# Four value tiles of the first batch by SyncE as f32, the first scores in a new order, and the first unit's output steps regrouped

## The chip, the cores and the metric

The kernel runs on one core of one Trainium2 chip. The metric is the device time of one execution in microseconds (us); of the kernel before there are 4 runs, 260.92 to 262.25 us, median 261.1 us. A profile is one such execution recorded instruction by instruction. Its engines are PE (TensorE matmul; PEld is its weight load), DVE (VectorE), ACT (ScalarE), POOL (GpSimd) and SP (SyncE, which here only issues DMAs). L103 is line 103 of the kernel before.

## The reference, cut to what matters

Shapes: q, k, v are (4 batches, 8 heads, 768 positions, 64), all f32.

```
k_sum = max  of k over blocks of 32 positions      (24 summary keys)
v_sum = mean of v over blocks of 32 positions      (24 summary values)
scores_l = q k^T / 8          only where |i - j| < 16
scores_s = q k_sum^T / 8 + log(32)
a = softmax over [scores_l, scores_s] together
attn = a [v ; v_sum]  ->  x: (3072 tokens, 512)
out = x + sigmoid(x w_res) * ((gelu(x w_gate) * (x w_val)) w_out)
```

w_gate and w_val are 512x1536, w_out 1536x512, w_res 512x512. Matmuls take bf16 operands.

## The kernel before, in words

**Units.** A unit is half a batch: 384 tokens. There are 8 units, u = 0 to 7. Work is issued in the order in which the code stands; there is no scheduler that would move it, and each engine works through its own instructions in that order. An instruction that waits holds up everything behind it on its engine.

**Attention on tiles of 64 positions.** `vext` (L78) holds for each of the 12 tiles of a batch 96 rows that go with its 64 queries (64 own values, 16 after, 16 before) and 32 more rows for the block means; columns D to VP of a tile (64 to 95) hold a column of ones for the softmax sum and zeros. `kW` (L75) holds the matching keys and `qT` the queries, both with the 64 features on partitions. `s_step` (L289) makes the scores of one pair of heads and their exponentials P; `av_step` (L312) multiplies P by `vext`; `xt_step` (L342) turns the result into `xT`, the operand of the dense layers. A pair of heads is "hp", 0 to 3.

**Dense part.** `fo_step` (L371) makes one of 12 column blocks of gate and value products on PE (lines 357 to 361, 4+4 matmuls of 128x384), gelu on ACT (L365), the product on DVE (L366). `res_step` (L394) makes a residual product for 128 tokens and its tanh on ACT; `ffn_step` (L403) the product with w_out, in parts over fo; `end_step` (L423) joins them and stores. The output steps of unit u are interleaved with the attention of unit u+1: in `first_out` (L521) for unit 0, `mid_out` (L553) for the others. w_gate and w_val come in 6 chunks of 256 columns each, so a chunk serves two fo.

**The start.** POOL loads with a cast from f32 to bf16, in this order: two halves of the keys (`k_sb`, L88), the first queries (`q_sb`, L96), 6 value tiles, four mask instructions (L176), 6 more value tiles (L103), then the weights (L189, L190, with the second queries L192 after the fifth pair), w_res, two shifted copies within `vext` (L194), w_out in three parts (L198), and the next batch. POOL has at most 8 such loads open: the compiled order shows each one waiting for the landing of the eighth before it. PE turns keys and queries (L205), ACT copies them out of PSUM (L237, L244), DVE forms the block maxima and the shifted rows of `kW` (L222 to L231). PE runs `keep_warm` (L437), matmuls on a dummy tile, where it would otherwise have nothing to do. `vsum_mm` (L247) makes the block means of the first batch on PE from all 12 value tiles, two matmuls a tile, spread between the score steps (lines 461 to 465); `vblk` (L466, L468) takes them. ACT's first work is to fill the pad columns of `vext[0]` (L168), DVE fills those of `vext[1]` (L182).

**Later batches.** `vsum_grp` (L254) makes the means on PE, DVE copies them to `vpart`, four small DMAs on SP move them to the rows of `vsum` (L264), and POOL spreads them over `vext` (L270). `turn_q` (L130) is a transposing DMA on SP.

`unit0_extras` (L505) is housekeeping done on DVE between the fo steps of unit 0. The order of the first scores reads:

```
        s_step(0, 0, st)
        q_place(0, 3, tq[3])
        s_step(0, 1, st, MM2)
...
        vsum_mm(0, vs, 0, 3)
        s_step(0, 2, st)
        vsum_mm(0, vs, 3, 5)
        s_step(0, 3, st, MM2)
        vsum_mm(0, vs, 5, NT)
```

Of the kernel before, what the change touches and what calls it, by code (L numbers as in the profile page):

```python
# [8 lines left out]
F32 = mybir.dt.float32  # L9
# [6 lines left out]
def kernel(  # L16
# [84 lines left out]
    def v_loads(b, lo=0, hi=NT):  # L101
        for t in range(lo, hi):
            nc.gpsimd.dma_start(out=vext[b % 2][0:QT, t, :, 0:D],  # L103
                                in_=v[b, :, t * QT:(t + 1) * QT, :].rearrange("h p d -> p h d"))
# [30 lines left out]
    with tc.manual_schedule():  # L135
# [13 lines left out]
        def own_keys(m, n):  # L149
            nc.vector.memset(m[:], 0.0)  # L150
            for i in range(2):
                rows = m[i * BLK:(i + 1) * BLK]
                nc.vector.memset(bass.AP(tensor=m.tensor, offset=rows[:, 0, i:i + 1].offset,
                                         ap=[rows.ap[0], [34, n]]), 1.0 / BLK)

        nc.vector.memset(warm[:], 0.0)
        nc.vector.memset(ident[:], 0.0)
        nc.vector.memset(bias_t[:], 0.0)
# [6 lines left out]
                                base=0, pattern=[[-1, 128]], channel_multiplier=1)  # L165
        load_k(0, k_sb[0], 1, 2)
        q_sb[0] = load_q(0, QJ)
        nc.scalar.activation(vext[0][0:QT, :, :, D + 1:VP],  # L168
                             warm[0:QT, 0:1].unsqueeze(1).unsqueeze(1).to_broadcast([QT, NT, H, VP - D - 1]),
                             AF.Copy)  # L170
        vext_consts(0)
        v_loads(0, 0, 6)
        for cols, sign, base in ((slice(0, QT), 1, WIN - 1), (slice(0, QT), -1, WIN - 1),
# [1 line left out]
            m = mneg[0:QT, cols]  # L175
            nc.gpsimd.affine_select(out=m, in_=m, compare_op=ALU.is_ge, fill=-240000.0, base=base,  # L176
                                    pattern=[[-sign, cols.stop - cols.start]], channel_multiplier=sign)
        v_loads(0, 6, NT)
        kw_consts(0)
        own_keys(bmat, NT)  # L180
        nc.vector.memset(vblk[96:128, :, D:D + 1], 1.0)
        nc.vector.memset(vext[1][0:QT, :, :, D + 1:VP], 0.0)  # L182


        wg_src = moe_w_gate.rearrange("(ko ki) f -> ki ko f", ki=128)
# [58 lines left out]
            nc.scalar.copy(qT[0][:, 3 * half:3 * half + 3, hp].rearrange("d c (p j) -> d c p j", j=qj),  # L244
                           tp.rearrange("d j (c p) -> d c p j", c=3))

        def vsum_mm(b, vs, lo, hi):  # L247
            for t in range(lo, hi):
                for i in range(2):
                    nc.tensor.matmul(vs[i][96:128, 0:DM // 2], bmat[:, t, :],  # L250
                                     vext[b % 2][0:QT, t, 4 * i:4 * i + 4, 0:D],
                                     start=(t == 0), stop=(t == NT - 1))

        def vsum_grp(b, pool, tag):  # L254
            vs = pool.tile([128, DM], F32, tag=tag, name="vs")
            for i in range(3):
                for g in range(4):
                    nc.tensor.matmul(vs[32 * g:32 * g + 32, :], bgrp[:, i, :],  # L258
                                     vext[b % 2][0:QT, 3 * g + i, :, 0:D],
                                     start=(i == 0), stop=(i == 2), tile_position=(0, 32 * g),  # L260
                                     skip_group_check=True)
            nc.vector.tensor_copy(vpart[:], vs[:])
            for g in range(4):
                nc.sync.dma_start(out=vsum[b % 2][96 + 6 * g:102 + 6 * g, :],  # L264
                                  in_=vpart[32 * g:32 * g + 6, :])

        def vsum_bc(b, lo, hi, eng):
# [169 lines left out]
        def keep_warm(n):  # L437
            wp = ps_s.tile([128, 2, 512], F32, tag="s", name="wp")
            for _ in range(n):
                nc.tensor.matmul(wp[:, 0], warm[:, 0:128], warm[:], start=True, stop=True)  # L440
# [4 lines left out]
        keep_warm(6)  # L445
        k_step(0, 2, ps_mm, "mm")
        k_step(0, 3, ps_mm, "mm")
        keep_warm(5)
        tq = [turn_pair(q_sb[0], hp, turn_tile(q_sb[0], ps_mm, "mm")) for hp in range(NP)]
        for hp in range(3):  # L450
            q_place(0, hp, tq[hp])
        keep_warm(1)
        st = new_unit()
        vs = [ps_t.tile([128, 512], F32, tag="t", name="vs"), ps_o.tile([128, 512], F32, tag="ao", name="vs")]
        s_step(0, 0, st)
        q_place(0, 3, tq[3])
        s_step(0, 1, st, MM2)
        x = vext[0]
        nc.vector.tensor_copy(x[QT:BAND, 1:HT, :, 0:D], x[QT - 2 * WIN:QT, 0:HT - 1, :, 0:D])
        nc.vector.tensor_copy(x[QT:QT + WIN, 0:HT, :, 0:D], x[0:WIN, 1:HT + 1, :, 0:D])  # L460
        vsum_mm(0, vs, 0, 3)
        s_step(0, 2, st)
        vsum_mm(0, vs, 3, 5)
        s_step(0, 3, st, MM2)
        vsum_mm(0, vs, 5, NT)
        nc.vector.tensor_copy(vblk[96:128, 0:H // 2, 0:D],  # L466
                              vs[0][96:128, 0:DM // 2].rearrange("p (h d) -> p h d", d=D))
        nc.scalar.copy(vblk[96:128, H // 2:H, 0:D],  # L468
# [36 lines left out]
        def unit0_extras(fo):  # L505
            if fo == 2:
                mt = ps_o.tile([128, 128], BF16, tag="ao", name="mt")
                nc.tensor.transpose(mt[:], mneg[:], ident[:])
                nc.vector.tensor_scalar(out=maskt[:], in0=mt[:, 0:QT], scalar1=-1.0, scalar2=None,
                                        op0=ALU.is_ge)  # L510
                own_keys(bgrp, 3)
            elif fo == 3:
                kw_consts(1)
            elif fo < 7:
                vsum_bc(0, 2 * fo - 2, 2 * fo, nc.vector)
            elif fo == 7:
                vext_consts(1)
            elif fo < 10:
                nc.vector.memset(vsum[fo - 8][96:128, :], 0.0)

        def first_out(u, st, gvT, nst):  # L521
            n = u + 1
            other = dict(pool=ps_t, tag="t")
            turn = dict(pool=ps_t, tag="t", copy=nc.scalar.copy)
            s_step(n, 0, nst)
            s_step(n, 1, nst, TO2)
            res_step(st, 0)
            res_step(st, 1)
            ffn_step(st, gvT, 0, 0, 4)
            av_step(n, 0, nst)  # L530
            av_step(n, 1, nst, **other)
            s_step(n, 2, nst)
            ffn_step(st, gvT, 1, 0, 4)
            res_step(st, 2)
            ffn_step(st, gvT, 2, 0, 4)
            xt_step(n, 0, nst, **turn)
            av_step(n, 2, nst)
            s_step(n, 3, nst)
            ffn_step(st, gvT, 0, 4, 8)
            ffn_step(st, gvT, 1, 4, 8)  # L540
            xt_step(n, 1, nst, **turn)
            ffn_step(st, gvT, 2, 4, 8)
            av_step(n, 3, nst)
            xt_step(n, 2, nst, **turn)
            ffn_step(st, gvT, 0, 8, FO)
            end_step(u, st, 0)
            ffn_step(st, gvT, 1, 8, FO)
            xt_step(n, 3, nst, **turn)
            ffn_step(st, gvT, 2, 8, FO)
            end_step(u, st, 1)  # L550
            end_step(u, st, 2)
# [39 lines left out]
        for u in range(NU):  # L591
            b, half = u // 2, u % 2
            nb = b + 1
            if half == 0 and nb == 1:
                k_sb[nb] = k_tile()
                load_k(nb, k_sb[nb], 0, 1)
                v_loads(nb)
                load_q_nat(nb)
            if u:
                gvT = upool.tile([128, FO, TU], BF16, tag="gvT", name="gvT")  # L600
            for fo in range(0 if u else 2, FO):
                if u > 1 and fo == 0:
# [12 lines left out]
                if half == 0 and 1 < nb < B and fo == 0:  # L615
                    pool_after(st["xT"][0:1, KO - 1, 0:1])
                    k_nat = load_k_nat(nb)
                    v_loads(nb)
                if half == 0 and b and fo == 1:
                    v_rims(b, HT, NT)  # L620
                if half == 0 and 1 < nb < B and fo == 6:
                    turn_k(nb, k_nat)
                    k_rims(nb, slice(0, NP), nc.gpsimd)
                if half == 1 and nb < B:
                    if fo == 0:
                        v_rims(nb, 0, HT)
                        if nb > 1:
                            pool_after(st["xT"][0:1, KO - 1, 0:1])
                            load_q_nat(nb)
                    if fo == (4 if nb == 1 else 1):  # L630
                        vsum_grp(nb, ps_t, "t")
                        for i in range(4):
                            vsum_bc(nb, 3 * i, 3 * i + 3, nc.gpsimd)
                        turn_q(nb, 0)
                        turn_q(nb, 1)
                    if nb == 1:
                        if fo == 0:
                            tk = turn_all(k_sb[nb])
                        if fo < NP:
                            k_place(nb, fo, tk[fo])  # L640
                    elif 2 <= fo < 2 + NP:
                        k_blocks(nb, fo - 2)
            if u == NU - 1:
                last_out(u, st, gvT)
            else:
                nst = new_unit()
                (mid_out if u else first_out)(u, st, gvT, nst)
                st = nst
# [30 lines left out]
```

## Time and profile before

| what | value |
|---|---|
| time of 4 runs | 260.92 to 262.25 us, median 261.1 us |
| time of the profiled execution | 260.92 us |
| its span, first to last instruction | 259.0 us |
| PE busy | 249.8 us (96%) |
| DVE, ACT, POOL busy | 156.2, 126.0, 104.3 us |
| granted TensorE clock | 0.996 |
| mean DMA rate | 114 GB/s (29.61 MB) |

The 1.92 us between time and span lie around the recorded instructions. PE is busy for 96% of the span, but that counts the dummy matmuls of `keep_warm`, so a busy PE in the first 21 us isn't a PE with useful work. The rows of a timeline read: start in us, duration in us, engine, line, operation, output<-inputs, how many instructions are merged in the row, and in brackets the idle time of the engine before the row with what ended it. In the rows by stretch each engine's busy time stands beside its name, then the granted clock, then "DMA share" (above 1, several packets lie in one DMA engine at once) and the rate.

### The profile page before, as it was taken

The numbers are of one execution on the slowest core, as the hardware profiler recorded it, in microseconds if no ns is written. First come the engines' busy times: TensorE is split into PE (matmuls) and PEld (weight loads), VectorE is DVE, ScalarE is ACT, GpSimd is POOL, SyncE is SP. The second block draws the span as 40 slices with busy tenths as digits, with TensorE's granted clock in tenths as the row PEclk, the third lists the DMA queues.
The fourth block names the chain that finished last, engine by engine and source line by source line (L and its number), as shares of the span: only waits on it lengthen the run. The fifth ranks groups of instructions, "written<-read, shape, count | busy, mean of one in ns | idle before, by whom it ended". The sixth has DMA issues, their size and how long they took to land.

```text
span 259.0 us, 5828 instructions
## 1 busy us (share of the span) xinstructions
PE 249.8 (96%) x2306; PEld 138.6 (54%) x2306; DVE 156.2 (60%) x346; ACT 126.0 (49%) x210; POOL 104.3 (40%) x142
## 2 busy tenths in 40 slices
PE   6999997999999999999999999999999999999993
PEld 2565653565654565545654565546554665456543
DVE  5945763489568544667667544778666544854324
ACT  6685347556383437543393338343482337343310
POOL 8896454285170888243530987153620000000000
PEclk9999999999999999999999999999999999999998
DMA  5999999999943999979903999969803400240012
GB/s 83 177 121 170 197 215 206 199 166 173 90 91 62 178 128 136 123 133 168 142 0 65 200 116 151 113 130 164 134 16 107 104 0 3 48 138 0 0 40 85
DMA packets 98299, 29.61 MB, mean 114 GB/s; under 512 B 83384, under 2 KB 95104, under 8 KB 98160
## 3 DMA queue, kind: packets, MB, share of 16 engines
q0 software_dynamic: 68400, 14.96, 71.3%
q1 hardware_dynamic: 29872, 14.29, 25.0%
q8 instruction: 18, 0.29, 0.5%
q14 instruction: 9, 0.07, 0.1%
HBM read 29.36 MB, written 6.29 MB: 138 GB/s over the span
## 4 chain that ended last, share of the span: by engine, by line
PE 80%; DMA 11%; POOL 3%; ACT 2%; DVE 1%; issue 1%; POOLq 0%; DVEq 0%
PE f L408 23%; PE g L360 22%; PE vv L360 21%; PE r L398 7%; DMA w_val<-in_moe_w_val_dram 4%; DMA w_gate<-in_moe_w_gate_dram 3%; DMA q_sb<-in_q_dram 3%; PE ao L320 3%; PE s L284 2%; POOL vext L103 1%; PE vs L258 1%; DVE P L306 1%; DMA out_dram<-o 1%; ACT P L302 1%; POOL w_val L190 1%
## 5 line engine op out<-in xcount | busy, mean ns | idle before, releaser
L366 DVE TENSOR_TENSOR gvT<-ge,vv 128x384 bf16<-128x384 f32 x96 | 52.9, 553 | 50.9 <-PE vv L360 46.3
L365 ACT ACTIVATE ge<-g 128x384 f32<-128x384 f32 x96 | 47.0, 491 | 74.2 <-DVE gvT L366 41.3
L360 PE MATMUL vv<-xT,w_val 128*128 128x384 bf16 x384 | 78.8, 326 | 0.5 <-DMA w_val<-in_moe_w_val_dram 0.5
L360 PE MATMUL g<-xT,w_gate 128*128 128x384 bf16 x384 | 78.8, 326 | 0.3
L408 PE MATMUL f<-w_out,gvT 128*128 128x512 bf16 x276 | 64.9, 380 | 1.3 <-ACT th L401 1.3
L360 PEld LDWEIGHTS <-w_gate 128*128 128x128 bf16 x384 | 37.1, 98 | 26.5 <-issue 1.6
L360 PEld LDWEIGHTS <-w_val 128*128 128x128 bf16 x384 | 37.4, 98 | 25.6 <-DMA w_val<-in_moe_w_val_dram 1.1
L408 PEld LDWEIGHTS <-gvT 128*128 128x128 bf16 x276 | 25.7, 98 | 30.8 <-DMA w_out<-in_moe_w_out_dram 1.8
L103 POOL DMA_DIRECT2D vext<-in_v_dram x48 | 32.7, 724 | 13.2 <-DMA w_out<-in_moe_w_out_dram 5.7
L401 ACT ACTIVATE th<-r 128x512 f32<-128x512 f32 x24 | 13.6, 605 | 28.4 <-PE r L398 28.4
L414 DVE SCALAR_TENSOR_TENSOR th<-th,f 128x512 f32<-128x512 f32 (+2 forms) x26 | 16.7, 641 | 15.4 <-PE f L408 15.4
L270 POOL COPY vext<-vsum 32x1536 bf16<-32x1536 bf16 x12 | 17.1, 1464 | 21.7 <-DMA vsum<-vpart 21.7
L306 DVE TENSOR_TENSOR P<-P,maskt 128x768 bf16<-128x768 bf16 x28 | 16.7, 601 | 11.6 <-ACT P L302 7.0
L398 PE MATMUL r<-w_res,xT 128*128 128x512 bf16 x96 | 23.2, 380 | 0.4 <-DMA w_res<-in_moe_w_res_dram 0.4
L302 ACT ACTIVATE P<-s,bias_t 128x768 bf16<-128x768 f32 x17 | 15.3, 901 | 6.6 <-PE s L284 6.4
L340 DVE TENSOR_TENSOR xn<-ao,rz 128x384 bf16<-128x384 f32 x32 | 17.8, 558 | 1.1
L417 DVE SCALAR_TENSOR_TENSOR o<-th,xn 128x512 f32<-128x512 f32 (+2 forms) x26 | 17.4, 669 | 1.5 <-DMA out_dram<-o 0.6
L117 POOL DMA_DIRECT2D k_nat<-in_k_dram x24 | 16.4, 741 | 1.0 <-DMA k_nat<-in_k_dram 0.7
L123 POOL DMA_DIRECT2D q_nat<-in_q_dram x18 | 15.9, 911 | 0.8 <-issue 0.7
L299 ACT ACTIVATE P<-s,bias_t 128x384 bf16<-128x384 f32 x30 | 15.7, 578 | 0.3 <-PE s L284 0.3
L222 DVE TENSOR_REDUCE ks<-kW 128x24 bf16<-128x768 bf16 x16 | 15.1, 945 | 0.4 <-ACT kW L237 0.3
L398 PEld LDWEIGHTS <-xT 128*128 128x128 bf16 x96 | 8.9, 98 | 10.3 <-issue 0.3
(82 smaller groups left out, 164.8 us busy)
## 6 DMA issues: line engine op xcount, KB each, us to landing
out_dram<-o SPq DMA_DIRECT2D x23, 256.0 KB, 2.3
vext<-in_v_dram POOLq DMA_DIRECT2D x48, 64.0 KB, 6.4
q_nat<-in_q_dram POOLq DMA_DIRECT2D x18, 128.0 KB, 7.1
w_gate<-in_moe_w_gate_dram POOLq DMA_DIRECT2D x6, 256.0 KB, 8.7
w_val<-in_moe_w_val_dram POOLq DMA_DIRECT2D x6, 256.0 KB, 9.5
w_out<-in_moe_w_out_dram POOLq DMA_DIRECT2D x3, 512.0 KB, 12.4
k_nat<-in_k_dram POOLq DMA_DIRECT2D x24, 64.0 KB, 4.4
vext<-vext SPq DMA_DIRECT2D x6, 144.0 KB, 5.4
```

The source lines that it names most:

```text
L103: nc.gpsimd.dma_start(out=vext[b % 2][0:QT, t, :, 0:D], in_=v[b, :, t * QT:(t + 1) * QT, :].rearrange("h p d -> p h d"))
L270: eng.tensor_copy(vext[b % 2][96:128, lo:hi, :, 0:D], src)
L302: nc.scalar.activation(P.rearrange("p a t q -> p a (t q)"), s2[:, :, 0:TU], AF.Exp, scale=scale, bias=bias_t[:])
L306: nc.vector.tensor_mul(Pf, Pf, maskt.unsqueeze(1).to_broadcast([128, 2 * HT, QT]))
L340: nc.vector.tensor_mul(xn, ao[:, :, :, 0:D], rz.to_broadcast([128, NSUB, 2, D]))
L360: nc.tensor.matmul(ps[:, 0:TU], w[:, ko, fo * 128:(fo + 1) * 128], st["xT"][:, ko, :], start=(ko == 0), stop=(ko == KO - 1), skip_group_ch ...
L365: nc.scalar.activation(ge[:], g[:, 0:TU], AF.Gelu)
L366: nc.vector.tensor_mul(gvT[:, fo, :], ge[:], vv[:, 0:TU])
L398: nc.tensor.matmul(r[:], st["xT"][:, ko, ss], w_res[:, ko, :], start=(ko == 0), stop=(ko == KO - 1))
L408: nc.tensor.matmul(st["f", sub][:], gvT[:, fo, ss], w_out[:, fo, :], start=(fo == 0), stop=(fo == FO - 1), skip_group_check=True)
L414: nc.vector.scalar_tensor_tensor(th[:, cs], th[:, cs], 1.0, f[:, 0:n], ALU.add, ALU.mult)
L417: nc.vector.scalar_tensor_tensor(o.rearrange("p (k d) -> p k d", d=128), th[:, cs].rearrange("p (k d) -> p k d", d=128), 0.5, x, ALU.mult, ...
```

## The change

Seven edits, none of which alters what is computed:

1. Value tiles 8 to 11 of batch 0 are no longer loaded by POOL. SP loads them at the very start, as f32, into a new tile `v32` (tiles 8 and 10 in partitions 0 to 63, 9 and 11 in 64 to 127), with two DMAs of 256 KB. ACT copies tiles 8 and 10 into `vext[0]` as bf16, ahead of its first copy of keys; DVE copies 9 and 11, ahead of its first block maximum.
2. The pad columns of `vext[0]` are zeroed by DVE, from column D rather than D+1, instead of by ACT; DVE's fill of `vext[1]` moves from the start into unit 0, in two halves (fo 3 and 7), and two other fills move one fo later.
3. The block means start with tiles 8 to 11, ahead of the turning of the queries; two of five dummy matmuls there go. The other 8 tiles follow in two groups of 4.
4. The scores of head pairs 2 and 3 are issued one right after the other.
5. In `first_out` the three residual steps stand together after the first two score steps, and the three first parts of `ffn_step` after the next attention steps.
6. The small DMAs of `vsum_grp` are issued by POOL instead of SP.
7. `turn_q` is issued ahead of `vsum_grp`, and for batch 1 both come at fo 5 instead of 4.

```diff
+        v32 = qk.tile([128, 2, H, D], F32, tag="k_nat", name="v32")
+        for i in range(2):
+            nc.sync.dma_start(out=v32[:, i],
+                              in_=v[0, :, (8 + 2 * i) * QT:(10 + 2 * i) * QT, :].rearrange("h p d -> p h d"))
         nc.vector.memset(warm[:], 0.0)
...
-        nc.scalar.activation(vext[0][0:QT, :, :, D + 1:VP],
-                             warm[0:QT, 0:1].unsqueeze(1).unsqueeze(1).to_broadcast([QT, NT, H, VP - D - 1]),
-                             AF.Copy)
+        nc.vector.memset(vext[0][0:QT, :, :, D:VP], 0.0)
         vext_consts(0)
         v_loads(0, 0, 6)
...
-        v_loads(0, 6, NT)
+        v_loads(0, 6, 8)
+        nc.scalar.copy(vext[0][0:QT, 8:NT:2, :, 0:D], v32[0:QT])
         kw_consts(0)
         own_keys(bmat, NT)
         nc.vector.memset(vblk[96:128, :, D:D + 1], 1.0)
-        nc.vector.memset(vext[1][0:QT, :, :, D + 1:VP], 0.0)
+        nc.vector.tensor_copy(vext[0][0:QT, 9:NT:2, :, 0:D], v32[QT:2 * QT])
...
-                                     start=(t == 0), stop=(t == NT - 1))
+                                     start=(t == 8), stop=(t == 7))
...
-                nc.sync.dma_start(out=vsum[b % 2][96 + 6 * g:102 + 6 * g, :],
+                nc.gpsimd.dma_start(out=vsum[b % 2][96 + 6 * g:102 + 6 * g, :],
...
-        keep_warm(5)
+        vs = [ps_t.tile([128, 512], F32, tag="t", name="vs"), ps_o.tile([128, 512], F32, tag="ao", name="vs")]
+        vsum_mm(vs, 8, NT)
+        keep_warm(3)
...
-        vsum_mm(0, vs, 0, 3)
+        vsum_mm(vs, 0, 4)
         s_step(0, 2, st)
-        vsum_mm(0, vs, 3, 5)
         s_step(0, 3, st, MM2)
-        vsum_mm(0, vs, 5, NT)
+        vsum_mm(vs, 4, 8)
...
             elif fo == 3:
                 kw_consts(1)
+                nc.vector.memset(vext[1][0:QT, 0:HT, :, D:VP], 0.0)
             elif fo < 7:
                 vsum_bc(0, 2 * fo - 2, 2 * fo, nc.vector)
             elif fo == 7:
+                nc.vector.memset(vext[1][0:QT, HT:NT, :, D:VP], 0.0)
+            elif fo == 8:
                 vext_consts(1)
-            elif fo < 10:
-                nc.vector.memset(vsum[fo - 8][96:128, :], 0.0)
+            elif fo < 11:
+                nc.vector.memset(vsum[fo - 9][96:128, :], 0.0)
...
             s_step(n, 0, nst)
             s_step(n, 1, nst, TO2)
-            res_step(st, 0)
-            res_step(st, 1)
-            ffn_step(st, gvT, 0, 0, 4)
+            for sub in range(NSUB):
+                res_step(st, sub)
             av_step(n, 0, nst)
             av_step(n, 1, nst, **other)
             s_step(n, 2, nst)
-            ffn_step(st, gvT, 1, 0, 4)
-            res_step(st, 2)
-            ffn_step(st, gvT, 2, 0, 4)
+            for sub in range(NSUB):
+                ffn_step(st, gvT, sub, 0, 4)
...
-                    if fo == (4 if nb == 1 else 1):
+                    if fo == (5 if nb == 1 else 1):
+                        turn_q(nb, 0)
+                        turn_q(nb, 1)
                         vsum_grp(nb, ps_t, "t")
                         for i in range(4):
                             vsum_bc(nb, 3 * i, 3 * i + 3, nc.gpsimd)
-                        turn_q(nb, 0)
-                        turn_q(nb, 1)
```

More of the change, by code (lines that the diff above doesn't have):

```diff
@@ L245, in q_place, with vsum_mm @@
                            tp.rearrange("d j (c p) -> d c p j", c=3))
-        def vsum_mm(b, vs, lo, hi):
+        def vsum_mm(vs, lo, hi):
             for t in range(lo, hi):
@@ L250, in vsum_mm @@
                     nc.tensor.matmul(vs[i][96:128, 0:DM // 2], bmat[:, t, :],
-                                     vext[b % 2][0:QT, t, 4 * i:4 * i + 4, 0:D],
-                                     start=(t == 0), stop=(t == NT - 1))
+                                     vext[0][0:QT, t, 4 * i:4 * i + 4, 0:D],
+                                     start=(t == 8), stop=(t == 7))
         def vsum_grp(b, pool, tag):
@@ L453 @@
         st = new_unit()
-        vs = [ps_t.tile([128, 512], F32, tag="t", name="vs"), ps_o.tile([128, 512], F32, tag="ao", name="vs")]
         s_step(0, 0, st)
```

## The prediction

> **What bounds the kernel now.** I began with the page's 40 slices, went on to the chain of work that ended last, and then to the timelines of POOL, ACT and PE in the first 55 us, where all edits but two lie.
>
> ```profile
> PE   6999997999999999999999999999999999999993
> DMA  5999999999943999979903999969803400240012
> ...
> 17.46 8.13 DMA w_gate<-in_moe_w_gate_dram
> 25.88 11.39 DMA w_val<-in_moe_w_val_dram
> 37.31 0.82 PE vv L360 x4
> ```
>
> From 6.5 to 65 us the DMA engines are full (slices 2 to 10), and the chain up to 37.31 us runs through the weight loads: the first unit goes at the pace of the DMA stream. After 57 us PE is dense and the chain is PE alone; nothing in the change shortens that. So what can be won is what PE waits for before 55 us. These rows of PE say what that is:
>
> ```profile
> 16.03 1.70 PE L250 MATMUL vs<-vext,bmat 64*32 64x256 bf16 x14
> 17.66 0.95 PE L332 MATMUL ao<-vext,P 96*64 96x65 bf16 x48
> ...
> 37.31 0.82 PE L360 MATMUL vv<-xT,w_val 128*128 128x384 bf16 x4 [0.50 <-DMA w_val<-in_moe_w_val_dram]
> 40.24 1.89 PE L398 MATMUL r<-w_res,xT 128*128 128x512 bf16 x8 [0.35 <-DMA w_res<-in_moe_w_res_dram]
> 43.45 1.04 PE L408 MATMUL f<-w_out,gvT 128*128 128x512 bf16 x4 [1.32 <-ACT th L401]
> ```
>
> The first attention product starts when 14 block-mean matmuls are through; the last value chunk lands at 37.26, w_res at 40.20, the first w_out at 43.40 (landing times of the trace), each just as PE asks for it. And POOL says when that stream begins:
>
> ```profile
> 10.59 3.40 POOL L103 DMA_DIRECT2D vext<-in_v_dram  x5 [0.93 <-DMA q_sb<-in_q_dram]
> 13.94 1.01 POOL L189 DMA_DIRECT2D w_gate<-in_moe_w_gate_dram  x1
> ```
>
> Value tile 7 waits for q_sb to land (10.30), each tile then costs 0.68 us of issue, and the weights come behind tile 11.
>
> **Part 1: the weight stream.** Four tiles less are 4 x 0.68 = 2.7 us of POOL: w_gate's first issue goes from 13.94 to 11.26. Not all of it reaches the stream, since tiles 6 and 7 still have to pass: tile 6 lands at 13.26, tiles land 0.43 us apart, so weight packets start near 13.6 instead of 15.5. I take 2.0 us, with 2.7 as the upper end; the lower end is 0, if v32 costs the engines elsewhere what four tiles cost (4 x 0.43 = 1.7 us).
>
> **Part 2: what v32 costs.** The trace has no f32 load by SP, so I bound it. The room:
>
> ```profile
> 2.00:4.00 2.00, 2.00 (x6) 0.76 (x5) 1.65 (x17) 1.99 (x2) 1.88 (x5) 1.00 0.30 28
> 4.00:6.00 2.00, 1.40 (x6) 0.39 (x4) 1.10 (x5) 0.71 (x1) 2.00 (x4) 1.00 1.19 192
> ...
> out_dram<-o SPq DMA_DIRECT2D x23, 256.0 KB, 2.3
> q_sb<-in_q_dram POOLq DMA_DIRECT2D x2, 384.0 KB, 9.3
> qT<-q_nat SPq DMA_TRANSPOSE x6, 3.9
> ```
>
> Before 4 us the engines carry next to nothing (share 0.30, 28 GB/s), from 4 us on 192 GB/s of bf16. SP starts at about 0.8 us. The two DMAs are 2048 packets of 256 B; the fastest value packets of this trace pass at about 590 in 0.5 us, so 1.7 us. Landing is bounded below by the store's 2.3 us and above by the first q_sb's 7.14 us; nearest is the transposing qT<-q_nat, also some 2000 packets of 256 B, with 3.9. With the second issue behind the first that gives L, the time at which v32 is there, as 3.3 to 8.3 us; I take 5.0.
>
> [...]
>
> **Part 3: who waits for v32.** In the compiled order of the changed kernel ACT's table load waits for a v32 landing, the copy behind it for the other, and the copies of keys stand behind both:
>
> ```profile
> 0.74 1.28 ACT L168 ACT_TABLE_LOAD   x1 [0.74 <-PEq L663]
> 2.03 2.68 ACT L168 ACTIVATE vext<-warm 64x2976 bf16<-64x2976 bf16 x1
> 7.03 1.50 ACT L237 COPY kW<-tp 128x768 bf16<-128x768 bf16 x2 [2.32 <-PE tp L205]
> ```
>
> The load is 1.28 us; the copy of 1024 f32 a partition I estimate from L299 and L302 (384 in 0.58, 768 in 0.90) at 1.1. ACT is free for keys at L + 2.4 = 7.4, 0.4 us late. Behind it the block maxima of DVE run dense from 7.86 to 13.54, then the shifted copies L459 and L460 to 15.70; the attention product that needs them comes at 17.0 in the new order, so 1.3 us are free. Cost: nothing up to L = 5.95, then 1 us for each us. DVE itself: the u32 fill of vext[0] (1536 elements at L182's 2.54 us for 2976: 1.3) pushes the start-up fills to about 6; its v32 copy is 0.5 to 1.1 and starts near 6, done by 7.1, before 7.86. In unit 0 the two halves of the vext[1] fill add 0.65 us at fo 3 and fo 7; DVE has 0.3 to 0.7 us free in each 1.3 us step and PE's four PSUM tiles give it another step: nothing. Uncovered it would be 1.3.
>
> [...]
>
> **Part 4: the first scores.** Eight block-mean matmuls (0.116 us each, 14 in 1.62) go ahead of the queries, two dummies (0.21) go: the turning starts at 11.05 instead of 10.65, as PE and no longer q_sb's landing sets it. Behind the scores 16 remain instead of 24: -0.93. Net: +0.40 - 0.93, and -0.12 for the split around pair 2, together **-0.65**: the attention product starts at 17.0. ACT's exponentials end at 17.3 (pair 3), in time for its product at 17.7.
>
> **Part 5: unit 0.** At 21.3 PEld waits 0.26 for the first w_val, landed at 21.22; 2 us earlier that wait is gone: **-0.25**. At the loop's end there are 0.25 before the turning of q_sb, 0.21 for the last w_gate and 0.68 until vv at 37.31 (37.31 - 36.63); with PE 0.9 earlier and the stream 2.0 earlier nearly all goes: **-0.9**.
>
> **Part 6: first_out.** PE idles 0.35 for w_res and 1.32 for the tanh. In the new order (all 1.8 us earlier) s starts at 37.55, w_res is there at 38.2, three residual steps of 0.865 last to 40.85. ACT has its table load from 37.5, exponentials to 40.65; DVE has masked pair 1 by 41.26, where PE waits 0.2; then s, and f at 41.9, with w_out there at 41.4. Idle 0.4 in place of 1.67: **-1.3**. What is late next is the second w_out (44.0, wanted at 45.3): in time.
>
> **Part 7: batch 1 and after.** The block means of batch 1 leave DVE at about 62.8; four POOL issues (0.52 each, L109's row, to 0.7) end at 65.1 and land near 68.2, 3.1 later (the shortest vext load under light use took 3.2). Two spreads of 1.43 us and the next attention product, then at 73.1, has its rows at 71.1. Free: 2 us. The queries of unit 2 need q_nat's third chunk (66.70 - 2.0) plus 3.9: 68.6, wanted at 69.9; behind vsum on SP they came at 68.99 + 3.9 before, so this gets safer. Batches 2 and 3: SP's 2.95 us of small issues become POOL's behind the q_nat issues; the spread ended at 131.6 for a product at 133.8. Nothing.
>
> **Sum:** -0.65 - 0.25 - 0.9 - 1.3 = -3.1. From 260.92 that is 257.8; the median of the runs lies 0.2 above the profiled execution, so 258.0 as a median.
>
> **Rivals.**
> - *The stream isn't earlier* (v32 delays keys, queries and tiles by what the four tiles took). Then parts 4 and 5 end in the same landings, and part 6 alone stays, since its idle time is filled by work, not by data: f starts at 43.7 with 1.64 us more of work done: 259.6. For it: 192 GB/s from 4 us on. Against it: the idle engines before. 17%.
> - *v32 is late, and ACT holds the keys* (slower). Price L - 5.95; it cancels the 3.1 at L = 9.05 and is slower by 1.3 from 10.35. If a 256 B packet took the 97 ns of the 1 KB ones at 4 to 6 us, 128 on each engine at share 1.25 are 9.9 us, L = 12 and the time 258.0 + 6.0 = 264. For it: an unseen kind of load, a table load behind it, and keys in the same engines. Against it: packets of 128 B at 590 per 0.5 us. 10%.
> - *The block means of batch 1 come late by POOL*: if the small DMAs take 6.4 us (the median vext load) the rows are there at 74.4 for 73.1: 259.2. 8%.
> - The edits do what they say in the compiled order; that they don't is left out.
>
> **How the numbers follow.** Forecast 55%, its own range 257.2 to 258.9 (stream 2.7 down to 1.2 us earlier); stronger, 6%, down to 256.5; several of the small margins gone, 4%, at 260.2 to 262. I place 256.8 to 260.5, which leaves out the late v32 and most of the last. Half a per cent, 1.3 us, is what a measurement of this kernel can tell. Faster by more: 0.77 (forecast, stronger, most of the third rival, half of the first). Within: 0.15. Slower: 0.08.
>
> **What would show it.** Right: v32 landed by 6 us, L237's successor at about 7.4, first w_gate issue near 11.3, the attention product at 17.0, no DMA wait on PE from 21 to 38 us, the first row of unit 1's g at 51.6 instead of 54.76. Wrong: q_sb landing well after 10.7, ACT idle before the keys "<-DMA v32", PE waiting for w_res or w_out as before.

## The result: 0.27% slower, where 1.2% faster was forecast

The changed kernel takes 262.45 us (median of 34 runs, 260.28 to 271.25), the kernel before 261.64 us beside it (55 runs, 260.44 to 262.48): ratio 1.0027, 95% interval 1.0015 to 1.0038, some 0.7 us slower. Four runs of 264.45 to 271.25 us, at granted clocks of 0.946 to 0.984, are left out of the ratio. The profiled execution took 263.23 us (span 261.1), 0.8 above the median, while that of the kernel before (260.92) lies 0.7 under its own; the two traces differ by 2.3 us where the medians differ by 0.8, and what follows says which is meant. The profiled execution's clock is 0.986, where 21 of 35 runs show 0.990 to 0.993.

The page of the changed kernel, in slices of 6.5 us:

```profile
PE   6699999999999999999999999999999999999994
PEclk9689999999999999999999999999999999999999
DMA  6999999999911699959902999949903500230003
```

The 6 and the 8 in slices 2 and 3 of PEclk are new: before, the clock was full there. From slice 4 on it is full again. The weight loads have left the chain of waits (DMA 11% and POOL 3% of the span before, DMA 4% now); its longest DMA piece is now the load of the keys, 7.42 us from 1.31 on. PE's timeline at the start:

```profile
8.78 1.49 PE L208 MATMUL tp<-ident,k_sb 96*64 96x96 bf16 x32 [3.12 <-DMA k_sb<-in_k_dram]
10.20 2.74 PE L443 MATMUL wp<-warm 128*128 128x512 bf16 x6
12.87 1.49 PE L208 MATMUL tp<-ident,k_sb 96*64 96x96 bf16 x32
...
16.30 0.87 PE L208 MATMUL tp<-ident,q_sb 96*64 96x96 bf16 x32
...
22.34 0.95 PE L335 MATMUL ao<-vext,P 96*64 96x65 bf16 x48
```

The same rows of the kernel before:

```profile
6.46 0.87 PE L205 MATMUL tp<-ident,k_sb 96*64 96x96 bf16 x32 [1.06 <-DMA k_sb<-in_k_dram]
7.26 1.47 PE L440 MATMUL wp<-warm 128*128 128x512 bf16 x6
...
10.65 0.87 PE L205 MATMUL tp<-ident,q_sb 96*64 96x96 bf16 x32
```

PE waits 3.12 us for the keys (1.06 before), then does the same 32 transposes in 1.49 us instead of 0.87, and six dummies in 2.74 instead of 1.47: half clock. The queries are turned at 16.30 (before 10.65), the attention product stands at 22.34 (17.66; forecast 17.0). The stretches of 2 us show why; the last three numbers are granted clock, DMA share and GB/s:

```profile
2.00:4.00 2.00, 2.00 (x6) 0.76 (x5) 1.39 (x2) 0.00 (x0) 1.88 (x5) 1.00 1.04 225
4.00:6.00 2.00, 1.66 (x6) 0.49 (x4) 1.70 (x17) 0.00 (x0) 2.00 (x3) 1.00 0.91 133
6.00:8.00 2.00, 0.00 (x0) 0.00 (x0) 0.28 (x4) 0.16 (x1) 1.41 (x3) 1.00 1.16 184
8.00:10.00 2.00, 1.23 (x32) 1.23 (x32) 0.56 (x1) 1.99 (x2) 0.94 (x2) 0.52 1.33 199
10.00:12.00 2.00, 2.00 (x13) 0.78 (x8) 1.06 (x2) 1.57 (x3) 1.21 (x4) 0.50 1.88 174
...
14.00:16.00 2.00, 2.00 (x21) 1.19 (x17) 1.37 (x4) 1.26 (x2) 2.00 (x4) 0.77 1.16 84
```

v32 went for the most part where the prediction put it: SP's queue passes 1765 packets from 2 to 4 us, at 225 GB/s. But from 4 to 6 us only 133 GB/s flow, against 192 before. POOL's queue, which holds the keys, passes 198 packets there instead of 391, beside 256 that are left of SP's (the last one at 7.2 us), and the key stream reaches its full pace (80 packets of 1 KB in half a microsecond) at 6.0 instead of 4.0. The two halves of the keys land at 8.73 and 10.70 (6.42 and 8.34 before), the queries at 12.69 (10.30). ACT and POOL:

```profile
7.84 1.28 ACT L181 ACT_TABLE_LOAD   x1 [7.84 <-DMA v<-in_v_dram]
9.13 1.04 ACT L181 CAST vext<-v 64x1024 bf16<-64x1024 f32 x1
10.09 1.48 ACT L240 COPY kW<-tp 128x768 bf16<-128x768 bf16 x2
```

```profile
12.98 0.68 POOL L103 DMA_DIRECT2D vext<-in_v_dram  x1 [1.31 <-DMA q_sb<-in_q_dram]
13.65 0.77 POOL L192 DMA_DIRECT2D w_gate<-in_moe_w_gate_dram  x1
```

ACT has the key copies 0.4 us late on top (the second half's copy starts 0.89 us behind its transposes, at 13.76; by that the first would start at 9.67); and POOL, each of whose loads waits until the eighth before it has landed, waits 1.31 us for the late queries with value tile 7, so the first weight load is issued at 13.65, only 0.3 before the old 13.94. Two of the signs that the prediction named for its own failure are there: queries landing well after 10.7, and ACT idle for v32 ahead of the keys.

**One account carries the rest.** Take the first row of each unit's gate products (g). From the first g of unit 0 to that of unit 1, PE has 31.2 us of work; what is more is waiting. The changed kernel has next to none left in unit 0, so whatever PE loses before its first g reaches the end in full.

| kernel (profiled) | first g of unit 0 | unit 0 takes | first g of unit 1 | unit 1 takes | clock |
|---|---|---|---|---|---|
| before | 21.30 | 33.46 | 54.76 | 31.12 | 0.996 |
| changed | 25.98 | 31.24 | 57.22 | 31.19 | 0.986 |
| e1_out, edit 5 alone | 21.27 | 31.97 | 53.24 | 31.57 | 1.000 |
| e4_nov32, all but v32 | 21.58 | 32.14 | 53.72 | 32.25 | 1.000 |
| e6_warm24, 24 dummies | 23.70 | 31.24 | 54.93 | 32.31 | 0.997 |

Units 2 to 6 take the same time in all five, but for e6_warm24's profile (1.3 us more); from the first g of unit 7 to the end are 30.0 to 30.4 us. Before, unit 0 held 2.2 us of waits. Edit 5 alone removes 1.5 of them, and 0.8 are left for an earlier weight stream to win. v32 costs 2.4 to 4.7 us of start for those 0.8 (1.4 in the best trace of any kernel with it, e12_warm_sp).

### The profile page after: what moved, and what is told of

It is laid out like the page before. It is cut to its first block, busy times and chain, and to the rows that moved or that the text cites. A ratio compares the mean times of both kernels' runs of the same rounds, so it can differ in the third digit from the quotient of the medians.

```text
span 261.1 us, 5827 instructions
## 1 busy us (share of the span) xinstructions
PE 252.1 (97%) x2304; PEld 140.1 (54%) x2304; DVE 156.7 (60%) x349; ACT 124.0 (47%) x210; POOL 108.4 (42%) x150
## 4 chain that ended last, share of the span: by engine, by line
PE 90%; DMA 4%; ACT 3%; DVE 1%; issue 1%; DVEq 0%; POOLq 0%
PE g L363 24%; PE f L411 23%; PE vv L363 23%; PE r L401 6%; DMA k_sb<-in_k_dram 3%; PE ao L323 3%; PE s L287 3%; PE tp L208 2%; PE wp L443 2%; PE vs L253 1%; ACT L305 1%; PE vs L261 1%; DMA out_dram<-o 1%; DVE P L309 1%; ACT P L302 1%; ACT P L305 1%
## 5 line engine op out<-in xcount | busy, mean ns | idle before, releaser
L103 POOL DMA_DIRECT2D vext<-in_v_dram x44 | 30.0, 723 | 15.5 <-DMA k_sb<-in_k_dram 5.9
L273 POOL COPY vext<-vsum 32x1536 bf16<-32x1536 bf16 x12 | 17.8, 1522 | 12.5 <-DMA vsum<-vpart 12.5
```

The costliest lines, as they stand in the source:

```text
L103: nc.gpsimd.dma_start(out=vext[b % 2][0:QT, t, :, 0:D], in_=v[b, :, t * QT:(t + 1) * QT, :].rearrange("h p d -> p h d"))
L273: eng.tensor_copy(vext[b % 2][96:128, lo:hi, :, 0:D], src)
```

## The experiments

The theory after the result: v32, in front of the keys, delays them; PE's idle time then halves the clock; this eats what edit 5 gains. The rivals: ACT's table load or the edits around batch 1 cost the time, or the clock alone does. Each expectation names the theories that it sets apart; A is the one held at the time. Ratios are to the kernel before, beside each run.

**e1_out: edit 5 alone on the kernel before.**

```diff
-            res_step(st, 0)
-            res_step(st, 1)
-            ffn_step(st, gvT, 0, 0, 4)
+            for sub in range(NSUB):
+                res_step(st, sub)
...
+            for sub in range(NSUB):
+                ffn_step(st, gvT, sub, 0, 4)
```

> The kernel before with the regrouped output steps of unit 0 alone (edit 5). Theory A (the regrouping fills PE's waits for w_res, tanh and w_out; the loss of the whole change comes from the start): 1.3 to 1.7 us faster than before, from s of unit 1 at 39.4 to g of unit 1 at 53.1 to 53.4 instead of 54.8. Rival C (the regrouping only moves the wait): within 0.3 us of before.

260.33 us, ratio 0.9963 (0.9942 to 0.9983). PE's timeline:

```profile
40.19 2.75 PE L398 MATMUL r<-w_res,xT 128*128 128x512 bf16 x12 [0.33 <-DMA w_res<-in_moe_w_res_dram]
...
43.68 2.76 PE L408 MATMUL f<-w_out,gvT 128*128 128x512 bf16 x12
...
53.24 0.81 PE L360 MATMUL g<-xT,w_gate 128*128 128x384 bf16 x4
```

The 1.32 us that PE waited for the tanh before its first f are gone, w_res's 0.33 stay; unit 1 starts 1.5 us earlier. That is the gain of the whole change, and it was kept to the end: this kernel is 1.0 us faster (1.3 to 1.7 expected).

**e2_load: the kernel before, with v32 loaded and nothing reading it.**

```diff
+        v32 = qk.tile([128, 2, H, D], F32, tag="k_nat", name="v32")
+        for i in range(2):
+            nc.sync.dma_start(out=v32[:, i], in_=v[0, :, (8 + 2 * i) * QT:(10 + 2 * i) * QT, :]...)
```

> The kernel before plus the two f32 loads of SP and nothing that reads them; POOL still loads all 12 value tiles, so 0.5 MB more is moved. Theory A (the loads' packets take the DMA engines from 2 to 4.5 us, keys and queries land 2.3 us later, PE idles 3.1 us and its clock falls to half): keys land near 8.7 and 10.7, queries near 12.7, granted clock near 0.5 between 9 and 14 us, and the time is 3 to 5 us over before. Rival B (what costs is ACT's and DVE's wait for the loads, ahead of the copies of keys): no engine waits for them here, so the time is within 1 us of before and the clock stays at 1.0.

263.81 us, ratio 1.0091 (1.0059 to 1.0122). Keys land at 8.83 and 10.80, queries at 13.14:

```profile
8.88 1.36 PE L209 MATMUL tp<-ident,k_sb 96*64 96x96 bf16 x32 [2.73 <-DMA k_sb<-in_k_dram]
```

```profile
10.00:12.00 2.00, 2.00 (x11) 0.77 (x8) 1.50 (x5) 1.13 (x2) 1.25 (x5) 0.50 1.75 170
```

PE waits 2.73 us and the clock falls to 0.50 from 10 to 12 us. No ACT table load waits here and no edit is made: the load by itself does it. The time is 2.4 us over, under theory A's 3 to 5; it also holds half a megabyte more that has to pass ahead of the weights.

**e5_half: the same with one of the two loads** (`range(1)`).

> The kernel before plus one of the two f32 loads (256 KB) that nothing reads. With both, the first keys landed at 8.83 instead of 6.42. Theory A (what holds the keys up is the number of packets ahead of them): half the delay, first keys near 7.6, queries near 11.4, PE idle 1.5 to 2 us at the keys, the granted clock stays at 1.0, and the time is 0.8 to 1.6 us over before. Rival D (a fixed price of any early SP load): keys as late as with both, 8.7 or more, and the clock falls.

262.69 us, ratio 1.0049 (1.0032 to 1.0066). Keys land at 7.35 and 9.29, 0.9 late; the clock stays at 1.00. Its stretches:

```profile
2.00:4.00 2.00, 2.00 (x6) 0.76 (x5) 1.65 (x17) 1.99 (x2) 1.88 (x5) 1.00 0.80 146
4.00:6.00 2.00, 1.75 (x6) 0.50 (x4) 1.10 (x5) 0.71 (x1) 2.00 (x4) 1.00 1.06 154
```

By 3.3 us the last v32 packet is through. Still the keys have 154 GB/s from 4 to 6 us, not 192. So it isn't that v32 reached into the keys' time: what came first slowed the start of what came next. And the load costs time with a full clock too, here with 256 KB more to pass ahead of the weights.

**e4_nov32: the changed kernel without edits 1 and 3 and with the old score order** (all 12 tiles by POOL; v32, its loads and its copies go).

> The changed kernel without the f32 loads, its two copies and its new order of the first scores (edits 1, 3 and 4 undone; 2, 5, 6 and 7 stay; POOL loads all 12 tiles). Theory A: keys land at 6.4 and queries at 10.3 as before, clock 1.0 and 1.2 to 1.8 us faster than before. Rival C (the means of later batches by POOL's queue cost what the regrouping wins): within 0.5 us of before, with PE waiting for POOL near 73 us.

260.51 us, ratio 0.9957 (0.9939 to 0.9976); keys at 6.42, clock 1.00. That is 1.1 us under the kernel before (1.2 to 1.8 expected). Taking v32 and what hangs on it out of the changed kernel gains 1.8 us (0.0070 of 261.6). So v32, with what it brings on, is the loss, and the rest is as good as edit 5 alone.

**e3_warm and e6_warm24: the changed kernel with 28 and 24 dummies at the start instead of 12**, so that PE has no idle time while the keys are late.

```diff
-        keep_warm(12)
+        keep_warm(28)
```

> The changed kernel with 28 dummy matmuls at the start instead of 12, which cover PE up to about 8.8 us, where the first keys land. Theory A: no drop of the granted clock, keys as late as in the changed kernel, the queries turned near 13.5 instead of 16.3; 260.0 to 261.0 us, about 1.8 us under the changed kernel. Rival B (the clock only follows, the late copies of keys set the pace): not more than 0.5 us under the changed kernel.

> The changed kernel with 24 dummy matmuls at the start instead of 12; with 28 they lasted to 9.1 us, 1.0 beyond the landing of the keys. Theory A (the granted clock is a price of its own, about 2.5 us of PE from 8.8 to 16 us, and 28 were one us too many): clock 1.0, queries turned near 13.0, 261.2 to 261.8 us. Rival E (at full clock PE only waits for the same data, so the clock costs nothing): as with 28, 262.0 to 262.5.

262.23 us, ratio 1.0032 (1.0014 to 1.0049), and 261.83 us, ratio 1.0011 (0.9993 to 1.003). PE of e6_warm24:

```profile
1.19 8.17 PE L443 MATMUL wp<-warm 128*128 128x512 bf16 x24 [1.19 <-DVE warm L160]
9.29 0.87 PE L208 MATMUL tp<-ident,k_sb 96*64 96x96 bf16 x32
```

The clock is 1.00 in every row, 32 transposes are back at 0.87, and the first g comes at 23.70 instead of 25.98, though the keys landed only 0.3 earlier (8.43). The dummies last until 9.29, so 0.9 is given away; with 28 it is 1.0 (9.13 for keys at 8.09), and theory A's 260.0 to 261.0 us for 28 were missed. In the medians 24 dummies win 0.4 us (0.0016 of 261.6; the intervals overlap).

That is not all that the clock is worth, since PE starts late here. The runs of the changed kernel itself show more: of 35, 4 have a clock of 1.000 and took 260.28 to 261.28 us (median 260.7); 21 have 0.990 to 0.993 and a median of 262.4; 10 have 0.986 or less and took 262.93 us or more. e8_sp's runs, below, fall apart in the same way (260.81 and 260.92 at 1.000, 262.6 or more at less). So with the clock kept the change is 0.9 us faster than the kernel before, as edit 5 alone is, and the half clock seems to carry most of v32's price. Against it stands that e6_warm24 and e12_warm_sp keep the clock too and lie near 261.7, which dummies that outlast the keys explain only in part. What spared the four runs no trace shows; their keys may have come earlier too. A candidate: a dummy takes 0.43 us at first and 0.21 later (from 4.2 us on in the kernel before), and when that changes differs from trace to trace. The first 12 dummies last 4.09 us in e13_big and 5.30 in e4_nov32, and the longer they last, the shorter PE idles.

**e7_late: e1_out with v32 started behind POOL's sixth value tile; all four copies on DVE, behind the shifted rows; w_out's loads stand behind them in the code.**

```diff
+        for i in range(2):
+            nc.gpsimd.memset(v32[0:1, i, 0, 0:1], 0.0)
...
+        nc.vector.tensor_copy(x[0:QT, 8:NT:2, :, 0:D], v32[0:QT])
+        nc.vector.tensor_copy(x[0:QT, 9:NT:2, :, 0:D], v32[QT:2 * QT])
```

> The kernel before with edit 5 and with the two f32 loads, which SP now starts behind POOL's sixth value tile (about 8 us); DVE copies all four tiles behind the shifted rows of the first batch, and the block means keep their order. Theory A (the engines are one resource: two loads cost the stream what four tiles cost): keys land at 6.4, clock 1.0, first w_gate packets no earlier than 15, and within 0.5 us of edit 5 alone (260.3). Rival F (the stream starts 2.0 us earlier, as predicted, once the keys are out of the way): 0.9 us or more under edit 5 alone.

265.6 us, ratio 1.0139 (1.0108 to 1.017). Both expectations missed the time. Keys and queries are on time (6.46, 10.35), and the last value chunk lands 2.4 us earlier (34.84). But the packets of v32 now take the place of POOL's value tiles: tile 6 lands at 16.99 instead of 13.26, and PE waits:

```profile
17.03 0.59 PE L251 MATMUL vs<-vext,bmat 64*32 64x256 bf16 x4 [0.57 <-DMA vext<-in_v_dram]
18.91 0.38 PE L251 MATMUL vs<-vext,bmat 64*32 64x256 bf16 x2 [1.29 <-DVE vext L462]
19.71 1.41 PE L251 MATMUL vs<-vext,bmat 64*32 64x256 bf16 x6 [0.42 <-DVE vext L463]
```

The clock then stays at 0.50 from 20 to 30 us, after waits none of which is over 1.29 us. Here too the load costs the neighbour that it is put beside.

**e8_sp: the changed kernel with edits 6 and 7 undone.**

```diff
-                nc.gpsimd.dma_start(out=vsum[b % 2][96 + 6 * g:102 + 6 * g, :],
+                nc.sync.dma_start(out=vsum[b % 2][96 + 6 * g:102 + 6 * g, :],
...
-                    if fo == (5 if nb == 1 else 1):
-                        turn_q(nb, 0)
-                        turn_q(nb, 1)
+                    if fo == (4 if nb == 1 else 1):
```

> The changed kernel with edits 6 and 7 undone (small DMAs on SP, at fo 4, queries turned behind them). Theory A (POOL's later spread costs DVE and PE in unit 1 only where PE comes early; in the changed kernel PE comes 2.5 us late and the wait is 0.2 us): within 0.4 us of the changed kernel. Rival C (edits 6 and 7 cost about 1.2 us in any kernel, as in the run without the f32 loads): 261.0 to 261.6 us.

263.05 us, ratio 1.0056 (1.0029 to 1.0082); unit 1 takes 31.24 us, as in the changed kernel. The ratio is 0.003 above the changed kernel's, and the intervals overlap. Edits 6 and 7 aren't the loss.

**e9_means: e1_out with edits 6 and 7.**

> The kernel of e1_out (the kernel before with edit 5) with edits 6 and 7 as well: the small DMAs of the block means by POOL, the turning of the queries first and, for batch 1, both one step later. PE is early here (attention product near 17.7 us, first g of unit 1 near 53.2), and nothing of v32 is in it. Theory A (edits 6 and 7 put POOL's spread of batch 1's means beside DVE's mask multiplies once PE is early, and cost what the run without v32 showed): unit 1 takes 32.2 to 32.8 us instead of 31.6, the first two mask multiplies of unit 2 about 3.3 us instead of 2.35, and the median lies 0.7 to 1.3 us above e1_out's, near 261.0 to 261.6. Rival (the loss in the run without v32 came from edits 2 or 4, the fills and the score order): unit 1 stays at 31.4 to 31.6 and the median within 0.3 us of e1_out's 260.3.

260.71 us, ratio 0.9978 (0.9964 to 0.9992). The trace shows what theory A said. POOL's spread of batch 1's means and DVE's mask multiplies, here and (second pair of fences) in e1_out:

```profile
71.83 6.35 POOL L270 COPY vext<-vsum 32x1536 bf16<-32x1536 bf16 x4 [4.08 <-DMA vsum<-vpart]
```

```profile
73.43 3.41 DVE L306 TENSOR_TENSOR P<-P,maskt 128x768 bf16<-128x768 bf16 x2 [0.81 <-ACT P L302]
```

```profile
69.02 5.70 POOL L270 COPY vext<-vsum 32x1536 bf16<-32x1536 bf16 x4 [7.39 <-DMA vsum<-vpart]
```

```profile
73.25 2.35 DVE L306 TENSOR_TENSOR P<-P,maskt 128x768 bf16<-128x768 bf16 x2 [1.02 <-ACT P L302]
```

A mask multiply takes 0.56 us alone. The two beside the spread take 3.41 together, PE waits 1.27 us for the second, and unit 1 takes 32.31 instead of 31.57. But the medians differ by 0.4 us from e1_out (0.0015 of 261.5; the intervals overlap), between what the two theories needed: the 0.7 us of the trace are not confirmed by the time.

**e12_warm_sp: e6_warm24 with edits 6 and 7 undone.**

> The changed kernel with 24 dummy matmuls at the start instead of 12 (as in e6_warm24) and with edits 6 and 7 undone (as in e8_sp). Theory A (undoing 6 and 7 gained nothing in e8_sp because PE was late there; with the clock kept at 1.0 PE is earlier, and then they cost): unit 1 near 31.2 us instead of e6_warm24's 32.3, the median 0.6 to 1.1 us under e6_warm24's, near 260.7 to 261.2, below the kernel before. Rival (edits 6 and 7 cost nothing in any form of the changed kernel): within 0.3 us of e6_warm24's 261.8.

261.65 us, ratio 1.0009 (0.9997 to 1.0022). In its trace, 260.83 us, the 24 dummies are done before the keys land at 8.28:

```profile
1.19 6.82 PE L443 MATMUL wp<-warm 128*128 128x512 bf16 x24 [1.19 <-DVE warm L160]
8.32 0.87 PE L208 MATMUL tp<-ident,k_sb 96*64 96x96 bf16 x32 [0.31 <-DMA k_sb<-in_k_dram]
```

Unit 1 takes 31.38 us instead of 32.31, yet the time is that of e6_warm24. Theory A falls on the time; in the changed kernel edits 6 and 7 cost nothing that can be measured.

**e10_turn and e11_best: e1_out with the turning of the queries ahead of the block means, both on SP** (edit 7's order without edit 6, at fo 4); the second also has edit 4.

> The kernel of e1_out with one thing of edit 7: the turning of the queries issued ahead of the block means, the small DMAs still on SP and both at fo 4 as before. In e1_out PE waited 0.36 us at 71.9 for the turned queries, which stood behind the means' DMAs on SP. Theory A: that wait goes, the spread by POOL starts later by what the transposing DMA's issue takes on SP, so it lies beside one more mask multiply: between 0.4 us faster and 0.8 slower than e1_out, the value taken 0.2 faster, 260.1. Rival (the order on SP matters to nobody, the wait moves to the next instruction): within 0.15 us of e1_out's 260.3.

> The kernel of e10_turn with edit 4: the scores of pairs 2 and 3 one after the other, the block-mean matmuls of tiles 0 to 2 ahead and 3 to 11 behind. Theory A (edit 4 saves the split around pair 2, 0.1 us, which the weight stream then takes back, since w_val of the first chunk lands when it did): within 0.15 us of e10_turn. Rival (the first attention product and all behind it 0.3 us or more earlier): 0.3 to 0.6 us faster than e10_turn.

266.54 us, ratio 1.0199 (1.0172 to 1.0225), and 267.06 us, ratio 1.022 (1.0204 to 1.0236). Every expectation for e10_turn missed the level, and e11_best, expected level with it or faster, is 0.5 us slower (the intervals overlap). SP and PE of e10_turn:

```profile
66.16 4.52 SPq L132 DMA_TRANSPOSE qT<-q_nat  x2
70.73 2.99 SPq L264 DMA_DIRECT2D vsum<-vpart  x4
```

```profile
76.62 0.26 PE L320 MATMUL ao<-vext,P 128*64 128x65 bf16 x5 [1.32 <-POOL vext L270]
78.03 0.48 PE L320 MATMUL ao<-vext,P 128*64 128x65 bf16 x19 [1.16 <-POOL vext L270]
```

The block means stand behind 4.5 us of turning on SP, the spread by POOL starts at 75.1 instead of 69.0, and PE waits for it in each batch: unit 1 takes 33.69 us, units 3 and 5 29.94 and 30.79 instead of 29.05. Edit 7 needs edit 6. Edit 4 leaves the attention product at 17.58, 17.56 without it: the 0.12 of Part 4 for the split isn't there.

**e13_big, e14_thin and e15_five: what the keys pay for.** The kernel before with loads that nothing reads: 512 KB in 256 packets; 256 KB in 2048 packets; v32 itself, but issued behind DVE's fills near 3.7 us.

```diff
+            nc.sync.dma_start(out=v32[:, i].rearrange("p h d -> p (h d)"),
+                              in_=moe_w_out[i * 128:(i + 1) * 128, :])
```

> The kernel before plus two loads by SP at the very start, nothing reads them: 512 KB as in e2_load, but rows of w_out, 2 KB each, so 256 packets in place of 2048. Theory P (what holds the keys back is the number of packets that SP's loads put in front): the first half of the keys lands 0.2 to 0.5 us later than the 6.42 of before, PE's first idle stretch stays under 1.6 us, the granted clock at 1.0, the time within 0.5 us of the kernel before. Theory B (it is the bytes): 2.0 to 2.6 us later, as in e2_load, PE idle near 3 us, the time 2 to 2.8 us above before.

> The kernel before plus two loads by SP at the very start, nothing reads them: half of each row of v32, so 2048 packets of 128 B, 256 KB. Theory P (number of packets): keys 2.0 to 2.6 us later than 6.42, time 2 to 2.8 us above the kernel before, as e2_load with as many packets. Theory B (bytes): keys 0.8 to 1.2 us later, time 1 to 1.5 us above, as e5_half with as many bytes.

> The kernel before plus both f32 loads of v32 by SP, nothing reads them, but started only behind DVE's fills of vext, near 3.7 us, when all key packets are queued and stream at full rate (before: from 4.0 us on). Theory F (what costs is that v32 stands in front of POOL's queue while that starts up): the first half of the keys lands within 0.8 us of 6.42, the second half and the queries up to 1.5 us late; the time 0.3 to 1.5 us above before. Theory S (the engines serve SP's packets ahead of or beside POOL's whenever they come, and the keys pay for the whole load): the first half 1.0 to 2.3 us late, second half and queries 2.0 to 2.5 us late as in e2_load, the time 2 to 3 us above before.

| kernel | load in front | keys land | queries | ratio (95% interval) |
|---|---|---|---|---|
| before | none | 6.42, 8.34 | 10.30 | |
| e5_half | 256 KB, 1024 packets | 7.35, 9.29 | 11.46 | 1.0049 (1.0032 to 1.0066) |
| e14_thin | 256 KB, 2048 packets | 8.04, 10.01 | 11.99 | 1.0043 (1.0027 to 1.006) |
| e13_big | 512 KB, 256 packets | 8.10, 10.71 | 12.70 | 1.0066 (1.0049 to 1.0083) |
| e2_load | 512 KB, 2048 packets | 8.83, 10.80 | 13.14 | 1.0091 (1.0059 to 1.0122) |
| e15_five | 512 KB, 2048 packets, behind the start of the keys | 6.59, 8.49 | 11.50 | 1.0097 (1.0082 to 1.0112) |

Theory P falls: 256 packets hold the keys back by 1.7 us, where it allowed 0.5; 2048 of the same bytes do by 2.4. Whether packets count beside the bytes stays open: at 256 KB twice the packets add 0.7 us, but the six traces with v32 itself in front have the first half of the keys anywhere from 8.09 to 8.84, so 0.7 between two single traces shows nothing. In e13_big, too, nothing of the load is left after 4 us and the keys come slowly after it:

```profile
2.00:4.00 2.00, 2.00 (x6) 0.76 (x5) 1.65 (x17) 1.99 (x2) 1.88 (x5) 1.00 0.88 255
4.00:6.00 2.00, 1.29 (x6) 0.39 (x4) 1.10 (x5) 0.71 (x1) 2.00 (x4) 1.00 0.94 111
```

e15_five didn't put v32 beside the keys: SP issues at 3.61, but v32's first packet passes at 8.09, when the keys' last one (8.05) is through. In front it took 1.1 us from issue to first packet (0.74 to 1.86), in e7_late 4.1 (8.10 to 12.21). The keys are on time, as theory F says, but the time is theory S's, since v32 passes beside the queries and the value tiles (116 packets of v32 to 125 of q_sb from 8.5 to 9 us): the queries are 1.2 us late, and PE's last 14 block-mean matmuls take 2.43 us instead of 1.70. Half a megabyte more in the first 17 us costs 1.7 to 2.5 us in all three kernels that have it.

## Why the prediction was wrong, point by point

- **Part 2 is the step that failed**: "Before 4 us the engines carry next to nothing", and therefore v32 at 5.0 and keys on time. Most of v32 passed in that time as forecast; the keys still came 2.3 us late (2.4 in e2_load, without any other edit), and 0.9 with half a load that was over at 3.3 us (e5_half). Even the four runs at full clock lie 2.7 us above the forecast of 258.0. The low rate ahead of the keys was not room here: loads that nothing reads, put there, made the keys 0.9 to 2.4 us late (e5_half, e14_thin, e13_big, e2_load), while v32, issued at 3.61 us, left them 0.2 late (e15_five). So the stream's own start-up seems to lie in it. L itself was 7.8 (5.9 and 5.8 in e3_warm and e6_warm24), inside the stated 3.3 to 8.3. Where a load by SP met POOL's queue, its neighbours paid: value tile 6 landed at 16.99 us instead of 13.26 in e7_late, the queries at 11.50 instead of 10.30 in e15_five. The first rival, which counts such a delay and nothing else, came to 259.6 and lies 2.85 us under the measured time as well: it has no term for a late start.
- **Not foreseen: the clock.** The sum has no term for it. PE's cover for the keys was 12 dummies, enough for keys at 6.4 and not for 8.7. 3.1 us of idle time halved the clock until nearly 15 us: 0.6 us more on each 32 transposes, 1.3 on six dummies. The 24 dummies win back 0.4 us in the medians and up to 2.3 in the profiled start (25.98 to 23.70); between the median of the changed kernel and its four runs at full clock are 1.75.
- **Part 1**, the stream 2.0 us earlier: 1.4 (last value chunk at 35.84 instead of 37.26). The way there failed: the first weight load went out 0.3 us earlier, not 2.7, as POOL waited for the late queries; the rest is what four tiles less leave to pass.
- **Part 3**: the terms held: ACT free of v32 at 10.1 for L = 7.8 (L + 2.4 = 10.2), copies of 1.04 (1.1) and 0.69 (0.5 to 1.1), the fill 1.34 (1.3). ACT held the keys 0.4 us, the rival's mechanism at under a quarter of the 1.8 that this L would cost with keys on time. In the chain of waits PE alone stands from 8.78 to 20 us, so this hold set no pace.
- **Part 4**: from the turning of the queries to the attention product 6.04 us, 5.95 forecast, 7.01 before. Right, on top of a turning 5.65 us late. One reading was wrong: before, q_sb had landed at 10.30 and PE turned it at 10.65 straight behind its dummies, so PE set that start already.
- **Part 5**: no DMA wait on PE from 26 to 57 us; unit 0's loop up to the residual product shrinks from 18.94 to 17.79, the forecast 1.15. But PE came so late that the stream had been in time anyway, so that this hit says little for the reasoning.
- **Part 6**: -1.3 forecast, -1.5 measured in e1_out's trace and -1.0 in its time. Right, and the only gain that reached the end.
- **Part 7**: nothing forecast, nothing measurable found (e8_sp, e12_warm_sp). The 2 us of slack were judged by the spread's end alone; that it lengthens DVE's masks was missed (two in 3.41 us in e9_means, 2.35 in e1_out).
- **Rivals**: the first (stream no earlier, 259.6) had the keys and queries late for the right reason, though the stream was 1.4 earlier, and left out PE: it let the delayed keys cost nothing before the stream. The second had the right sign, by another way: the keys were late in the DMA engines, not behind ACT.

What stays open: why the key stream runs at 111 to 154 GB/s from 4 to 6 us after a load that has already passed (e13_big, e5_half), how the loss divides between the late keys and the clock, and what spared the four runs at full clock.

## What to carry to other kernels

Before filling an idle stretch of the DMA engines, ask what that stretch is the start-up of: load something unread there and see when the first needed data lands (8.83 us instead of 6.42 in e2_load). Count from the first product to the next in PE's own work: what a stream can give back is only the waiting in that stretch (here 0.8 us after edit 5), and the rest of a late start (2.4 to 4.7 us with v32) was paid in full. When data that PE waits for can come later, its dummy work must grow with it, but no further: 24 and 28 dummies kept the clock at 1.00 where 12 did not, and outlasting the keys by 0.9 and 1.0 us gave that time back (e6_warm24, e3_warm).

## What the runs showed of the hardware

- Single idle times of PE of 1.06 us (before) and 1.64 (e5_half) left the clock at 1.00; with 2.49 (e14_thin), 2.73 (e2_load), 2.86 (e13_big) and 3.12 us (the changed kernel) it fell to 0.50, for up to 6 us from the next work on. In e7_late it fell to 0.50 with shorter ones close together, 0.57, 1.29 and 0.42 us; in e10_turn, with 1.32 and 1.16, the profiled execution's clock is 1.000. So no length of one wait decides in these traces. It differs between runs of one kernel too: 4 of 35 of the changed kernel have a clock of 1.000.
- After a load by SP in front, POOL's queue reached its full pace (80 packets of 1 KB in half a microsecond) only 1.2 us (e5_half, 4.5 for 3.3) to 2.7 us (e13_big, 6.5 for 3.8) behind the load's last packet. A load that SP issued while POOL's queue streamed passed its first packet 4.1 us (e7_late) and 4.5 us later (e15_five); then, in e15_five, the two passed about one packet each (116 to 125 from 8.5 to 9 us).
- A mask multiply of 0.56 us took 1.7 beside POOL's copies (two in 3.41 us, e9_means).
